# Gateloop attention and a low-rank mixer: the first pair's second layer by half products, three pairs' inputs turned by DMA, chunk products joined, a new order

## The chip, the cores and the metric

One core of one Trainium2 chip runs the whole kernel. The metric is the device time of one launch in microseconds (us); smaller is better. TensorE is PE, VectorE is DVE, ScalarE is ACT, GpSimd is POOL, and SyncE (SP) issues most of the DMAs.

## The reference

Attention first: per batch and head a complex state decays by a normalised gate and takes up k v at every time step; the output is q times the state's real part. Then the mixer: a product of low rank along the sequence is added, and a two-layer net with a relu is added to that.

```python
# q, k, v, a_re, a_im: (4, 8, 768, 48)      B, H, S, D
mag = np.sqrt(a_re * a_re + a_im * a_im)
scale = np.minimum(mag, 0.999) / (mag + 1e-06)
a_re_n, a_im_n = (a_re * scale, a_im * scale)
for t in range(S):
    new_re, new_im = ar * S_re - ai * S_im, ar * S_im + ai * S_re
    S_re, S_im = (new_re + kv, new_im)            # kv = k[t] v[t]
    y[:, :, t] = np.einsum('bhd,bhde->bhe', q[:, :, t], S_re)
x = y.transpose(0, 2, 1, 3).reshape(4, 768, 384)
h = x.transpose(0, 2, 1) @ U @ V                  # rank 32 along the sequence
u = x + h.transpose(0, 2, 1)
out = u + np.maximum(u @ w_ch1, 0.0) @ w_ch2      # 384 -> 1536 -> 384
```

## The kernel before

**Tiling.** The 768 time steps of each of the four batches are six chunks of 128 rows, 24 chunks in all; a group is two chunks. The mixer works on pairs of two chunks (256 rows), 12 pairs in all, numbered m = 0 to 11.

**Attention.** For each chunk `gates`, `angles` and `waves` turn the gate into decays; they are mostly PE prefix sums, ACT functions and DVE products. `prep` weighs q and k and turns them: chunks 0 to 5 by PE transposes, later ones in `cross`, where ACT splits the numbers into 16-bit halves, SP writes them to DRAM (L933) and a DMA transpose fetches them back (L934). `chain` holds the chunk's PE products: `products` (L956) within 64 rows, masked by DVE (L959); `state` (L976), which makes the state's increments; `inside` (L1005), the masked products with v; and `before` (L1013), q with the carried state, in two halves. `products` and `before` use one arrangement of the PE array, `state` and `inside` another, and the mixer's large matmuls the whole array. ACT copies the result to a tile `xo` of 128 x 384 (L1022, L1024). `again` (L665) loads the gate a second time for a check of its range: each chunk's a_re and a_im by a DMA of its own (L671), one ACT square, two DVE operations, whose outcome goes into the tile `low` (L661).

**Mixer.** In `mixer(m)`, once in each batch, `rank` (L1048) multiplies the six chunks by U, and for every pair `spread` (L1071) multiplies that by V and `mixed` adds it to xo on DVE. `turned` transposes each chunk on PE (L1087, three 128 x 128 transposes) and copies it to uT (L1091). Pair 0 is worked ahead: its first layer is made without the low-rank part (`up`, L1102) and then mended by `corrected` (PE L1142, DVE L1148, from a tile `more` that ACT copies). From pair 2 on, the first layer is `up_fewer` (L1214), a scheme with fewer products; its combined weights come from `combine` (DVE L1267) and its combined inputs from DVE additions L1186.

**Second layer.** Pair 0 uses `down` (L1303): for each of its two chunks 12 matmuls of 128x384, each of which needs one piece of w2, and one DVE addition. The others use `down_two` (L1346): with the rows and columns split into halves it takes seven half products instead of eight, 42 matmuls of 128x192, eight DVE sums over the hidden layer (L1338) and seven additions (L472), and it reads three differences of w2's halves. These three (W2S, DVE L652) can only be made when all of w2 has been converted from its 64-bit form (`single`, DVE L616, L624, L472). One half of w2 is overwritten by a difference, "turned w2" (L1416), ahead of the first pair's use of it.

**Order.** All operations are registered with a `Plan`; a hand-written table `ORDER` of their numbers then sets the order of issue on every engine. `SPARE` puts dummy matmuls (`idle`, L1506) before an operation, `WARM` others (`warm`, L1513). They write to banks that nothing reads yet. An engine works off its instructions strictly in this order.

Of the kernel before, what the change touches and what calls it, by code (L numbers as in the profile page):

```python
# [118 lines left out]
)  # L119

SPARE = {
    410: 3, 447: 1,
}

WARM = {
    112: (2, 1), 126: (1,), 136: (2, 2, 2, 2, 2, 2, 1), 141: (2,), 162: (2, 2, 2), 235: (2, 2, 2, 2, 1), 242: (2,), 245: (2,), 259: (2, 2, 1), 266: (1, 1, 1, 1, 1, 1, 1, 1, 1),
}

AIM = {}

DUMP = None

# [194 lines left out]
def kernel(  # L327
# [24 lines left out]
    KH = KF // 2  # L352
    DH = DM // 2

    PLAIN = 1
    NS = 5
    FEWER, SINGLE, AHEAD = 2, 3, 1
    NCH = S // CH
# [69 lines left out]
    def c_act(n):  # L428
        return 0.22 + 0.0008 * n
# [1153 lines left out]
```

## Time and profile before

| | us |
|---|---|
| median of 3 runs (lowest, highest) | 530.15 (529.94, 530.81) |
| the profiled execution, its time | 529.77 |
| its span, first to last instruction | 528.0 |

The profile lists for each engine the time it was busy as a share of the span, then the span in 40 slices, the DMA queues, the chain of work that ended last, and the costliest groups of instructions. The program's names in a row stand as output<-inputs. A matmul of 32-bit floats leaves two records in the trace, one for each of its passes, so the counts of PE records in the trace are twice the matmuls in the code. Where a time of one matmul is given it holds both. The table by windows gives the busy time of each engine within stretches of the span; a share of PE below the stretch's length is time in which PE stood still.

### The profile page before, as it was taken

The numbers are of one execution on the slowest core, as the hardware profiler recorded it, in microseconds if no ns is written. First come the engines' busy times: TensorE is split into PE (matmuls) and PEld (weight loads), VectorE is DVE, ScalarE is ACT, GpSimd is POOL, SyncE is SP. The second block draws the span as 40 slices with busy tenths as digits, with TensorE's granted clock in tenths as the row PEclk, the third lists the DMA queues.
The fourth block names the chain that finished last, engine by engine and source line by source line (L and its number), as shares of the span: only waits on it lengthen the run. The fifth ranks groups of instructions, "written<-read, shape, count | busy, mean of one in ns | idle before, by whom it ended". The sixth has DMA issues, their size and how long they took to land.

```text
span 528.0 us, 15692 instructions
## 1 busy us (share of the span) xinstructions
PE 509.3 (96%) x6670; PEld 460.3 (87%) x6670; DVE 414.5 (79%) x787; ACT 346.0 (66%) x555; POOL 31.6 (6%) x61
## 2 busy tenths in 40 slices
PE   4999999899999999999999999999999999999996
PEld 2777887666998997999999989999999989999996
DVE  4779897799989987898798797878796575958452
ACT  8899998998869978978896768843543313131100
POOL 1000000001010000101011000110000000000110
PEclk9999999999999999999999999999999999999998
DMA  9959958479999998999899958999897543333101
GB/s 226 173 115 270 209 115 191 140 138 217 197 215 244 216 215 145 204 217 202 205 198 227 210 144 175 170 242 229 192 217 178 108 90 61 76 60 61 39 32 35
DMA packets 280670, 87.06 MB, mean 165 GB/s; under 512 B 271288, under 2 KB 272784, under 8 KB 280592
## 3 DMA queue, kind: packets, MB, share of 16 engines
q1 hardware_dynamic: 278384, 81.63, 76.0%
q0 software_dynamic: 2208, 4.35, 2.4%
q8 instruction: 54, 0.88, 0.7%
q14 instruction: 24, 0.20, 0.1%
HBM read 43.03 MB, written 23.63 MB: 126 GB/s over the span
## 4 chain that ended last, share of the span: by engine, by line
PE 88%; ACT 5%; DMA 3%; DVE 2%; issue 1%; SPq 0%; ACTq 0%
PE down L1346 25%; PE few L1214 14%; PE bank L1214 11%; PE up L1102 6%; PE inner L956 4%; PE bank L1013 4%; PE bank L976 4%; PE down L1303 3%; PE bank L1005 2%; DMA gate<-F 2%; PE bank L1071 2%; PE bank L1087 2%; ACT gate L466 1%; PE bank L777 1%; PE bank L782 1%; PE bank L842 1%
## 5 line engine op out<-in xcount | busy, mean ns | idle before, releaser
L466 ACT ACTIVATE gate<-gate 128x768 f32<-128x768 f32 (+2 forms) x85 | 86.1, 1018 | 25.8 <-DMA gate<-in_a_im_dram 14.7
L1346 PE MATMUL down<-w,h 128*128 128x192 f32 x396 | 70.4, 328 | 0.0
L466 ACT ACTIVATE QK<-QKC 128x768 uint16<-128x768 uint16 (+1 forms) x72 | 58.5, 848 | 13.1 <-DVE QKC L469 7.9
L1346 PEld LDWEIGHTS down<-w,h 128*128 128x128 f32 x396 | 64.6, 190 | 1.2 <-issue 0.8
L469 DVE TENSOR_TENSOR QKC<-qk,cs 128x768 f32<-128x768 f32 x48 | 44.9, 952 | 1.0 <-ACT cs L466 0.6
L472 DVE TENSOR_TENSOR xo<-down,xo 128x192 f32<-128x192 f32 (+1 forms) x79 | 29.9, 385 | 14.3 <-PE down L1346 14.1
L1222 ACT COPY h<-few 128x512 f32<-128x512 f32 x35 | 20.2, 583 | 27.8 <-PE few L1214 27.6
L1222 ACT COPY h<-bank 128x512 f32<-128x512 f32 x25 | 14.3, 588 | 36.0 <-PE bank L1214 31.0
L1346 PE MATMUL down<-stage 128*128 128x192 f32 x198 | 37.2, 328 | 0.0
L1102 PE MATMUL up<-uT,w 128*128 128x256 f32 x144 | 33.8, 383 | 0.0
L1346 PEld LDWEIGHTS down<-stage 128*128 128x128 f32 x198 | 32.5, 190 | 0.3 <-issue 0.2
L1102 PEld LDWEIGHTS up<-uT,w 128*128 128x128 f32 x144 | 26.7, 190 | 4.9 <-issue 0.6
L1290 POOL DMA_DIRECT2D out_dram<-xo x32 | 18.5, 590 | 202.9 <-DVE xo L472 164.5
L463 ACT ACT_TABLE_LOAD x22 | 28.2, 1283 | 1.1 <-PEq L1567 0.7
L828 POOL DMA_DIRECT2D gate<-F x15 | 12.0, 797 | 274.7 <-DVE stage L616 86.3
L1226 DVE CUSTOM_DVE_ANT_1 h<-few,h 128x512 f32<-128x512 f32 x31 | 21.0, 686 | 8.8 <-PE few L1214 8.1
L1214 PE MATMUL few<-extra,w 128*128 128x128 f32 x216 | 27.8, 275 | 0.0
L956 PE MATMUL inner<-QK 112*64 112x64 f32 x768 | 27.5, 224 | 0.2 <-DVE AT L959 0.2
L466 ACT ACTIVATE cs<-F 128x384 f32<-128x384 f32 x48 | 24.4, 518 | 3.9 <-DVE F L851 3.7
L956 PEld LDWEIGHTS inner<-QK 112*64 112x64 f32 x768 | 24.5, 138 | 2.4 <-issue 0.8
L1214 PEld LDWEIGHTS few<-extra,w 128*128 128x128 f32 x216 | 26.3, 192 | 0.1
L466 ACT ACTIVATE es<-bank 128x384 f32<-128x384 f32 x44 | 18.4, 502 | 9.2 <-PE bank L777 8.2
(185 smaller groups left out, 1166.8 us busy)
## 6 DMA issues: line engine op xcount, KB each, us to landing
xd<-QK SPq DMA_DIRECT2D x36, 512.0 KB
gate<-in_a_re_dram SPq DMA_DIRECT2D x48, 192.0 KB
gate<-in_a_im_dram SPq DMA_DIRECT2D x48, 192.0 KB
stage<-in_moe_w_ch_dram SPq DMA_DIRECT2D x12, 768.0 KB
qk<-in_q_dram SPq DMA_DIRECT2D x24, 192.0 KB
qk<-in_k_dram SPq DMA_DIRECT2D x24, 192.0 KB
VP<-in_v_dram SPq DMA_DIRECT2D x24, 192.0 KB
out_dram<-xo POOLq DMA_DIRECT2D x12, 192.0 KB, 4.2
```

The lines of the kernel that those rows point to most:

```text
L463: ACT(1.37, rank, lambda: nc.scalar.preload_act_table_set(name), writes=[TABLE])
L466: return nc.scalar.activation(out=o, in_=i, func=f, **kw)
L469: nc.vector.tensor_tensor(out=o, in0=a, in1=b, op=OP.mult)
L472: nc.vector.tensor_tensor(out=o, in0=a, in1=b, op=OP.add)
L956: nc.tensor.matmul(out=get(*ps0)[r:r + HC, h], lhsT=k_of(h, r, HC), rhs=q_of(h, r, HC), start=True, stop=True, tile_position=(0, r))
L976: nc.tensor.matmul(out=get(*dk[r])[x:x + D, h], lhsT=get(*ks)[at, h, x // DP, 0:D], rhs=get(*VPi)[at, h], start=True, stop=True, tile_posi ...
L1013: nc.tensor.matmul(out=get(*y[u])[side(r, u), p], lhsT=q_of(h, r * HC, HC), rhs=get(*(mid_G if r else ("G", i - 1)))[:, h], start=False, s ...
L1102: nc.tensor.matmul(out=get(*ps)[:, e], lhsT=w1[:, f, (ff + e) * 128:(ff + e + 1) * 128], rhs=get(*uT)[:, f], start=(f == 0), stop=(f == KD ...
L1214: nc.tensor.matmul(out=get(*ps)[:, q], lhsT=w()[:, q * 128:(q + 1) * 128], rhs=v[0](), start=(n == 0 and q == 0), stop=True, skip_group_ch ...
L1222: ACT(c_act(n3 * CH) - 0.045, RU, lambda i=i, k=k: nc.scalar.copy(out=at(i, k), in_=get(*ps)), [ps], [o])
L1226: DVE(c_dve(n3 * CH), RU, lambda i=i, k=k: nc.vector._custom_dve(dve_ops.TENSOR_ADD_SAT, out=at(i, k), in0=get(*ps), in1=at(i, k), s0=math ...
L1346: nc.tensor.matmul(out=get(*to)[:, part], lhsT=x(j), rhs=y[:, j], start=(first and j == 0), stop=(j == KH - 1), skip_group_check=not first)
```

## The change

1. `PLAIN` goes from 1 to 0: pair 0's second layer is made by `down_two` as well.
2. `TURNED = (9, 10, 11)`: for the chunks of the last three pairs `across` takes the place of PE's transposes and ACT's copy. ACT splits xo into 16-bit halves (two operations a chunk, into one tile `XU` that all six chunks share in turn), SP writes 192 KB to DRAM, and a DMA transpose brings it back into uT.
3. `JOIN = 8`: from chunk 8 on, a chunk's `state` is issued in one piece with the chunk before's `inside`, and the chunk before's two `before` halves in one piece with the chunk's `products`. The first chunk of each batch is left out, and 14 are joined. The numbers of matmuls stay.
4. `again` loads a group's two chunks by one DMA for a_re and one for a_im, 24 in place of 48, with 768 floats in a row for each partition; before, the rows were of 48. `low` holds 16-bit numbers; that makes room for `XU`.
5. `spread` no longer reads uT; the transposes take its buffer.
6. `ORDER`, `SPARE` and `WARM` are new: nine single dummies in place of four, and fewer but wider ones in `WARM`.

Line numbers move: `down_two`'s matmuls are at L1406, its sums at L1398, W2S at L653, "turned w2" at L1476, `spread` at L1116, `up_fewer` at L1274, the `combine` of weights at L1327, its inputs at L1246, the write and the transpose of `across` at L1150 and L1151, the loads of `again` at L674, the dummies at L1562, L1566 and L1573.

```diff
-    5, 97, 96, 0, 1, 2, 3, 102, 99, 101, 103, 4, 104, 105, 106, 107, 98, 116, 100, 115, 117, 118, 119, 10, 154, 8, 111, 112, 16, 9, 230, 108, 231,
...
+    5, 96, 0, 1, 2, 3, 4, 97, 99, 101, 102, 103, 104, 105, 100, 115, 98, 116, 117, 106, 8, 9, 111, 107, 108, 118, 119,
...
 SPARE = {
-    410: 3, 447: 1,
+    388: 1, 410: 1, 416: 1, 462: 3, 669: 3,
 }
 WARM = {
-    112: (2, 1), 126: (1,), 136: (2, 2, 2, 2, 2, 2, 1), 141: (2,), 162: (2, 2, 2), 235: (2, 2, 2, 2, 1), 242: (2,), 245: (2,), 259: (2, 2, 1), 266: (1, 1, 1, 1, 1, 1, 1, 1, 1),
+    125: (3,), 136: (4, 4, 4, 1), 141: (2,), 162: (4, 4, 4, 2, 2), 167: (2, 2, 2), 187: (1,), 235: (2, 2, 2, 2, 1), 263: (2, 2, 1), 273: (2,),
 }
-    PLAIN = 1
+    PLAIN = 0
+    JOIN = 8
-    low = singles.tile([128, GC * DM], FP, name="low")
+    low = singles.tile([128, GC * DM], U16, name="low")
+    XU = singles.tile([128, 2, DM], U16, name="XU")
+    TURNED = (9, 10, 11)
# again
-        for (nm, src), i in ((a, i) for a in ((ar, a_re), (ai, a_im)) for i in range(lo, hi)):
-            SP(c_dma(DM), ("load", 30 + n), lambda nm=nm, src=src, i=i: nc.sync.dma_start(out=get(*nm)[:, i - lo], in_=rows(src, i)),
-               writes=[nm + (i,)])
+        for nm, src in ((ar, a_re), (ai, a_im)):
+            SP(c_dma(W), ("load", 30 + n), lambda nm=nm, src=src: nc.sync.dma_start(
+                out=flat4(nm), in_=src[b, :, c * CH:(c + hi - lo) * CH].rearrange("h t d -> h (t d)").rearrange("h (p m) -> h p m", m=W)), writes=[nm])
# chain
+        joined, joins = c > 0 and i >= JOIN, not last and i + 1 >= JOIN
...
+        if joined:
+            p_inside, p_in, p_y, p_befores, p_b, p_leaves, p_rooms, p_takes = pending.pop(i - 1)
+            p_rooms()
+            def fused_x():
+                state(0, H)
+                p_inside()
+            PE(1.3, RR, fused_x, [ks, VPi] + p_in, [dk[r] for r in parts_k] + p_y, way=3, steps=4 * H * len(parts_k) + 4 * H,
+               takes=[mid_G] + p_takes)
+            states(True)
+            def fused_y():
+                p_befores()
+                products()
+            PE(1.8, RR, fused_y, p_b + [QK], p_y + [ps0], takes=[ATi], way=1, steps=8 * H)
+            states(False)
+            kept()
+            p_leaves()
# mixer
-            PE(0.76, R0, products, [r, ("V", 0)] + [uT + ("kept",)] * (m >= AHEAD), ps, way=5, steps=8)
+            PE(0.76, R0, products, [r, ("V", 0)], ps, way=5, steps=8)
+            if m in TURNED:
+                across(cc, i, u)
+                return
-            PE(0.33, R0, turn, [u], [tr], steps=KD)
+            PE(0.33, R0, turn, [u], [tr], takes=[uT], steps=KD)
+        def across(cc, i, u):
+            xu, xv = ("xu", i), ("xv", i)
+            ring(xu, "xu", [XU])
+            buffer(xv, "XV", 6, [CH, DM], bass.MemoryType.DRAM)
+            for n in range(2):
+                ACT(c_act(DM), R0, lambda n=n: act(get(*xu)[:, n], get(*u).bitcast(U16).rearrange("p (m n) -> p m n", n=2)[:, :, n], AF.Copy),
+                    [u], [xu + (n,)])
+            SP(0.6, R0, lambda: nc.sync.dma_start(out=get(*xv).bitcast(U16), in_=get(*xu).rearrange("p n m -> p (n m)")), [xu], [xv])
+            SP(0.8, R0, lambda: nc.sync.dma_start_transpose(
+                out=get(*uT).rearrange("p f (c t) -> p f c t", c=MC)[:, :, cc].bitcast(U16),
+                in_=get(*xv).bitcast(U16).rearrange("t (n m) -> (t n) m", n=2)), [xv], [uT + (cc,)])
```

**DVE, around the three differences of w2** (L652 before, L653 after; w_77 and w_78 are w2, w_76 and, after, w_77 are w1). Before:

```order
L472 ISA w_77<-w_77,stage 128x1536
L469 TENSOR_TENSOR QKC_107<-qk,cs 128x16x48
L469 TENSOR_TENSOR QKC_103<-qk,cs 128x16x48
L652 TENSOR_TENSOR stage<-w_77 128x1152
L469 TENSOR_TENSOR qk<-qk,es 128x768
L836 CAST GS_96<-gate 128x384
L837 TENSOR_TENSOR GS_97<-gate,GS_96 128x384
L652 TENSOR_TENSOR stage<-w_77,stage 128x1152
L472 TENSOR_TENSOR xo<-down,xo 128x384
L736 ISA gate<-gate 128x768
L798 TENSOR_TENSOR least<-least,T_115 112x16
L652 TENSOR_TENSOR stage<-w_77,stage 128x1152
```

And now:

```order
L471 ISA w_78<-w_78,stage 128x1536
L653 TENSOR_TENSOR stage<-w_78 128x1152
L838 CAST GS_97<-gate 128x384
L839 TENSOR_TENSOR GS_98<-gate,GS_97 128x384
L653 TENSOR_TENSOR stage<-w_78,stage 128x1152
L853 SCALAR_TENSOR_TENSOR F<-F,bank_62 128x384
L653 TENSOR_TENSOR stage<-w_78,stage 128x1152
L468 TENSOR_TENSOR QKC_108<-qk,cs 128x16x48
L1398 TENSOR_TENSOR stage<-extra 128x384 x2
L468 TENSOR_TENSOR QKC_104<-qk,cs 128x16x48
L1398 TENSOR_TENSOR more<-stage,extra 128x384
L1398 TENSOR_TENSOR stage<-stage,extra 128x384
```

Behind the last converted piece of w2 there were eight other rows between it and the third difference; now there are three, and pair 0's first four sums follow soon after.

**PE, at pair 0's second layer** (extra holds its hidden layer, stage and more hold differences and sums). Before:

```order
L1303 MATMUL down<-w_77,extra 128x384 x6
L842 MATMUL bank_61<-GS_96,prefix_r 128x384
L842 MATMUL bank_61<-GS_97,prefix_r 128x384
L1303 MATMUL down<-w_77,extra 128x384 x14
```

And now, with the 12 rows ahead of the first wait for a difference:

```order
L1562 MATMUL bank_62<-ident 128x128 x3
L844 MATMUL bank_62<-GS_97,prefix_r 128x384
L844 MATMUL bank_62<-GS_98,prefix_r 128x384
L1162 MATMUL up<-uT,w_77 128x256 x6
L1406 MATMUL down<-w_78,extra 128x192 x12
L1406 MATMUL down<-stage,extra 128x192 x6
L1406 MATMUL down<-stage 128x192 x3
L1406 MATMUL down<-stage,more 128x192 x3
L1406 MATMUL down<-stage 128x192 x6
```

The matmuls that read stage need the differences and the sums; those that read w_78 and extra alone do not.

**PE, behind the last batch's `spread`** (few and bank are `up_fewer`'s outputs for pairs 8 and 9). Before:

```order
L1071 MATMUL bank_65<-r,V 128x192
L1346 MATMUL down<-w_77,h 128x192 x3
L1346 MATMUL down<-stage,h 128x192 x3
L1346 MATMUL down<-stage 128x192 x3
L1346 MATMUL down<-stage,h 128x192 x3
L1087 MATMUL bank_61<-ident,xo 128x128 x3
L1346 MATMUL down<-stage,more 128x192 x3
L1087 MATMUL bank_62<-ident,xo 128x128 x3
L1346 MATMUL down<-stage 128x192 x3
L1346 MATMUL down<-w_77,h 128x192 x6
L1214 MATMUL bank_63<-extra,w_76 128x128 x4
```

And now:

```order
L1116 MATMUL bank_62<-r,V 128x192
L1274 MATMUL few<-extra 128x128 x4
L1406 MATMUL down<-w_78,h 128x192 x9
L1406 MATMUL down<-stage,h 128x192 x3
L1406 MATMUL down<-w_78,h 128x192 x3
L1406 MATMUL down<-stage,h 128x192 x3
L1406 MATMUL down<-stage 128x192 x3
L1406 MATMUL down<-stage,more 128x192 x3
L1406 MATMUL down<-stage 128x192 x6
L1406 MATMUL down<-w_78,h 128x192 x3
L1406 MATMUL down<-w_78,stage 128x192 x3
L1406 MATMUL down<-w_78,more 128x192 x3
```

The whole second layer of pair 8, 42 matmuls, now stands between the last `spread` and pair 9's first layer, which follows it; the transposes are gone.

More of the change, by code (lines that the diff above doesn't have):

```diff
@@ L1015, in before, with befores, rooms, halves @@
                                      tile_position=(0, (r ^ u) * HC), skip_group_check=True)
-        PE(0.44, RR, inside, [VPi, ATi, mid_G] + ([("G", i - 1)] if c else []), y, way=3, takes=[xi], steps=4 * H)
+        def befores():
+            for r in range(0 if c else 1, 2):
+                before(r)
+        def rooms():
+            for r in range(2):
+                psum(y[r], "Y", [128, HH, D], [128, HH, CH])
+            buffer(xi, "xo", 8, [128, DM])
+        def halves(a):
+            return a.rearrange("p (a u d) -> p a u d", u=2, d=D)
@@ new lines, in leaves @@
+        def leaves():
+            ACT(c_act(HH * D) - 0.04, RR, lambda: nc.scalar.copy(out=halves(get(*xi))[:, :, 0], in_=get(*y[0])), [y[0]], [xi + (0,)])
+            for r in range(2):
+                ACT(c_act(HH * D) + 0.04, RR, lambda r=r: nc.scalar.copy(out=halves(get(*xi))[r * HC:(r + 1) * HC, :, 1],
+                                                                         in_=get(*y[1])[side(r, 1)]), [y[1] + (r,)], [xi + (r + 1,)])
+        b_in = [QK, mid_G] + ([("G", i - 1)] if c else [])
@@ new lines, in chain @@
+        psum(ps0, "A", [128, H, HC])
+        buffer(mid_G, "GM", 2, [DQ, H, D])
+        if not last:
+            buffer(G, "G", 2, [DQ, H, D])
+        for r in parts_k:
+            psum(dk[r], "Y", [128, H, D], [128, H, DP])
+        if joined:
[14 more added lines that the diff above has]
+            p_leaves()
+        else:
+            PE(0.947, RL, products, [QK], [ps0], takes=[ATi], way=1, steps=4 * H)
+            kept()
+            for h0 in (0, HH):
+                PE(0.443, RR, lambda h0=h0: state(h0), [ks, VPi], [dk[r] + (h0,) for r in parts_k], way=3,
+                   steps=4 * HH * len(parts_k),
+                   takes=[mid_G] + ([] if last else [G]))
+            states(True)
@@ L1017, in chain @@
+        if joins:
+            pending[i] = inside, y_in, y, befores, b_in, leaves, rooms, [xi]
+            return
+        rooms()
+        PE(0.44, RR, inside, y_in, y, way=3, takes=[xi], steps=4 * H)
         if c:
@@ L1019, in chain @@
         PE(0.467, RR, lambda: before(1), [QK, mid_G], [y[0] + (1,), y[1] + (1,)], way=1, steps=2 * H)
-        def halves(a):
-            return a.rearrange("p (a u d) -> p a u d", u=2, d=D)
-        ACT(c_act(HH * D) - 0.04, RR, lambda: nc.scalar.copy(out=halves(get(*xi))[:, :, 0], in_=get(*y[0])), [y[0]], [xi + (0,)])
-        for r in range(2):
-            ACT(c_act(HH * D) + 0.04, RR, lambda r=r: nc.scalar.copy(out=halves(get(*xi))[r * HC:(r + 1) * HC, :, 1],
-                                                                     in_=get(*y[1])[side(r, 1)]), [y[1] + (r,)], [xi + (r + 1,)])
+        leaves()
+    pending = {}
     def mixer(m, ahead=False):
@@ L1082, in turned @@
             u = ("xo", i)
+            if m in TURNED:
+                across(cc, i, u)
+                return
             tr = out_of("uTp", i, [128, KD, CH], [128, 4, CH])
```

51 lines of the change are left out of this document (22 added, 29 removed), and 171 rows, old and new, of the table ORDER.

## The prediction

> **What bounds the kernel now.** I read the page's busy times and its chain first, then windows, then the waits of PE. On the page, the share of each engine and the chain of work that ended last:
>
> ```profile
> PE 509.3 (96%) x6670; PEld 460.3 (87%) x6670; DVE 414.5 (79%) x787; ACT 346.0 (66%) x555; POOL 31.6 (6%) x61
> PE 88%; ACT 5%; DMA 3%; DVE 2%; issue 1%; SPq 0%; ACTq 0%
> ```
>
> The windows (length, then busy PE, PEld, DVE, ACT, POOL with their counts, granted clock, DMA share, GB/s), first three that make up the span, then four around the first pairs:
>
> ```profile
> 0.00:24.00 24.00, 15.64 (x80) 11.10 (x81) 14.18 (x31) 19.06 (x35) 1.94 (x14) 1.00 1.08 209
> 24.00:504.00 480.00, 474.46 (x6463) 430.52 (x6462) 389.56 (x734) 326.90 (x521) 28.09 (x44) 1.00 0.81 169
> 504.00:528.00 24.00, 19.17 (x132) 18.72 (x130) 10.80 (x23) 0.00 (x0) 1.60 (x3) 0.94 0.11 37
> ...
> 114.00:130.00 16.00, 16.00 (x150) 9.86 (x139) 15.20 (x24) 13.11 (x17) 1.35 (x2) 1.00 0.82 216
> 130.00:147.00 17.00, 17.00 (x130) 14.94 (x130) 16.34 (x27) 15.46 (x25) 0.78 (x1) 1.00 0.89 175
> 147.00:164.00 17.00, 15.89 (x296) 14.79 (x289) 15.20 (x32) 12.56 (x18) 1.91 (x3) 1.00 1.13 263
> 164.00:180.00 16.00, 15.97 (x263) 15.16 (x262) 15.26 (x30) 15.74 (x28) 1.07 (x2) 1.00 1.11 210
> ```
>
> PE bounds the middle 480 us: only 5.5 us of it are idle. The head (8.4 us idle) and the tail (4.8) are bound by something else. From 114 to 180 DVE is as full as PE (62.0 of 66 us), so there work given to DVE can cost what PE saves. Two of PE's waits (us in all, times, longest):
>
> ```profile
> PE up L1142 <- ACT more L1128: 2.1, 1, 2.1
> PE down L1346 <- DVE xo L472: 1.1, 1, 1.1
> ```
>
> Both, 3.2 us together, lie before 165 and are most of what a better order could win in the middle.
>
> **The first pair's second layer on PE.** Three pieces of the chain (start, length, count of records; a matmul is two records):
>
> ```profile
> 108.77 2.59 PE up L1102 x12
> ...
> 118.86 9.03 PE down L1303 x28
> ...
> 211.74 1.95 PE down L1346 x12
> ```
>
> A matmul of 128x384 takes 2 x 9.03/28 = 0.645 us, one of 128x192 takes 2 x 1.95/12 = 0.325. Removed are 24 x 0.645 = 15.48, added 42 x 0.325 = 13.65: **-1.83 us**.
>
> **Transposes.** From the timeline of PE (start, length):
>
> ```profile
> 431.63 0.49 PE L1087 MATMUL bank<-ident,xo 128*128 128x128 f32 x3
> 431.96 1.14 PE L1346 MATMUL down<-stage,more 128*128 128x192 f32 x6
> ```
>
> Three hold PE for 431.96 - 431.63 = 0.33 us, 0.11 each; by the row's own length, which the next row overlaps, 0.49/3 = 0.163. Eighteen fewer (72 to 54): **-2.0 us**, at most -2.9. ACT loses six copies and gains twelve splits, but in the last batch it has room.
>
> **Joining.** The number of matmuls stays; what falls is the number of changes between arrangements of the array, by my count of the orders from 153 to 143.
>
> ```profile
> 165.74 0.68 PE L1005 MATMUL bank<-VP,AT 64*64 64x48 f32 x32
> 166.35 0.67 PE L1013 MATMUL bank<-G,QK 112*64 112x48 f32 x16
> 166.85 0.64 PE L1013 MATMUL bank<-GM,QK 112*64 112x48 f32 x16
> 167.42 1.16 PE L1214 MATMUL few<-gate,w 128*128 128x128 f32 x8
> ...
> 416.76 1.15 PE L1005 MATMUL bank<-VP,AT 64*64 64x48 f32 x64
> 417.84 0.67 PE L1013 MATMUL bank<-GM,QK 112*64 112x48 f32 x16
> ```
>
> One block of 32 records lasts 0.61 us to the next start, a double block of 64 lasts 1.08, 0.14 less than twice 0.61; the second of the two L1013 halves, which leaves its arrangement, lasts 0.57, the first 0.50. So one change costs 0.07 to 0.14; with 0.10, ten make **-1.0 us** (-0.7 to -1.4). The price: `inside` of a chunk now goes out with the next chunk's `state`, so a chunk's output leaves a chunk later. From chunk 8 on the pairs stand far behind the chunks, and I take nothing for that.
>
> **Dummies.** Five more single ones. Three before (six records) held PE from 111.53 to 112.29:
>
> ```profile
> 111.53 0.83 PE L1506 MATMUL up<-ident 128*128 128x128 f32 x6
> 112.29 1.26 PE L1142 MATMUL up<-V,more 32*128 32x256 f32 x4
> 114.37 4.14 PE L1303 MATMUL down<-w,extra 128*128 128x384 f32 x12
> ```
>
> That is 0.25 each, at most +1.3. Most stand at the correction of pair 0, where PE waited 2.1 for ACT: I take 0. The new `WARM` lies in the head, where PE has 8.4 us free: 0. The sum on PE is -4.8.
>
> **DVE's side.** Pair 0 gains eight sums and its additions become halves. Does PE wait for the differences of w2? DVE's timeline:
>
> ```profile
> 115.14 0.41 DVE L1148 CUSTOM_DVE_ANT_0 extra<-up,extra 128x256 f32<-128x256 f32 x1
> ...
> 119.98 0.95 DVE L472 CUSTOM_DVE_ANT_0 w<-w,stage 128x1536 uint16<-128x1536 uint16 x1
> ...
> 128.28 1.35 DVE L652 TENSOR_TENSOR stage<-w,stage 128x1152 f32<-128x1152 f32 x1
> ```
>
> Before, the third difference ended at 129.63, long after pair 0's layer began at 114.37. In the new order, priced row by row, 3.55 us more PE work stands ahead of that layer, so it begins near 117.9. Its first 12 matmuls (3.9 us) need no difference, the next 6 need the third one (at 121.8), and those after them, at 123.75, the first sums, which DVE ends 4.1 us behind the third difference. So the third difference must end by 119.65. On DVE it now follows the last correction by 5.9 us of work (one conversion, three differences, three other rows). On PE 12 first-layer matmuls (2 x 2.59 by the chain's row), a `state` (0.87) and two prefix sums (0.46, both in rows further down), 6.5 us without dummies, stand between its last correction and the layer, so that correction ends near 111.4; DVE ran it up to 2.85 us late before (115.14 against 112.29). That gives 111.4 + 2.85 + 5.9 = 120.15, 0.5 late, and the six dummies that stand there now would take more than that anyway: I take 0. The upper bound is today's 129.63 less the 5.65 us of DVE rows that were moved behind it: 124.0, which would stop PE for 4.3 us.
>
> The next place is pair 2's first `few`, which reads a weight that DVE combines:
>
> ```profile
> 152.89 0.55 DVE L1338 TENSOR_TENSOR h<-h 128x384 f32<-128x384 f32 x1
> 153.36 0.55 DVE L1186 TENSOR_TENSOR extra<-uT 128x384 f32<-128x384 f32 x1
> ...
> 157.37 0.36 DVE L836 CAST GS<-gate 128x384 fp32r<-128x384 f32 x1 [1.59 <-DMA gate<-F]
> ...
> 159.17 0.68 DVE L1267 TENSOR_TENSOR w<-w,extra 128x512 f32<-128x512 f32 x1
> ```
>
> ```profile
> 161.46 0.94 PE L976 MATMUL bank<-VP,QKC 64*48 64x48 f32 x64
> 162.33 1.15 PE L956 MATMUL inner<-QK 112*64 112x64 f32 x32
> 163.41 0.62 PE L842 MATMUL bank<-GS,prefix_r 128*128 128x384 f32 x2
> 163.87 1.95 PE L1214 MATMUL few<-extra,w 128*128 128x128 f32 x16
> ```
>
> Today the weight ends at 159.85 and PE comes at 163.87: 4.0 us to spare. In the new order a whole chunk's products move behind this point (0.87 for `state`, 1.08 for `products`, 0.61 and 1.07 for the rest, from the rows above: 3.63), and 1.83 is saved, so PE comes at 158.4. DVE has eight sums (0.47 each by the starts) and five half additions (0.27, a little over half of that) more ahead, and about 1.8 us of other rows less: 159.85 + 3.3 = 163.1. If both hold, PE stands 4.7 us; if DVE's idle gaps close (50 - 46.74 = 3.3 in the windows from 114 to 164, 1.59 of it in the row above) it is 1.4; if they close further, nothing. I take the middle, **+2.2 us** handed back.
>
> **Turned inputs.** Is pair 9's input back in time? Rows of SP's timeline, its longest kind of wait (us in all, times, longest), and ACT's copy of 384 columns, whose mean of 476 ns stands for one split:
>
> ```profile
> 400.94 0.34 SPq L933 DMA_DIRECT2D xd<-QK  x1
> ...
> 405.08 4.71 SPq L934 DMA_TRANSPOSE QK<-xd  x2
> ...
> SPq L671 <- DVE low L661: 48.6, 10, 9.2
> ...
> L1091 ACT COPY uT<-bank 128x384 f32<-128x384 f32 x21 | 9.6, 476 | 16.3 <-PE bank L1087 16.3
> ```
>
> The write of 512 KB was followed by its transpose after 4.14 us; 192 KB is 3/8 of it, 1.6 us; a transpose is 3/8 of 2.36 to issue and, by the same share, some 2.5 us to land. Addition 0.55, two splits 1.0, write 1.6, the second chunk's splits 1.0 (they wait for the shared tile) and write 1.6, transpose 2.5, DVE's combined inputs 1.5 (nine additions, most of them a third of the one at 153.36): 9.7 us. On PE 4 `few` matmuls (eight records, 0.9 by the sixteen at 163.87) and 42 downs (13.65) stand in between, 14.6. Behind a write that waits for its split, SP holds only loads of `again` and the other turned chunks. So it is hidden; without that cover it would cost 9.7, once, since pairs 10 and 11 are turned in the shade of pair 9. The 24 fewer loads of `again` only free DMA engines and SP; nothing on PE's path waits for them.
>
> **The sum.** 529.77 - 4.8 + 2.2 = 527.2 for the profiled execution. The median lies 0.38 above that execution: **527.5 us**. The bounds: dummies +1.3, the hand-back 0 to 4.7, transposes -2.9, changes -0.7 to -1.4 give 525 to 530 for this case.
>
> **The rivals.**
>
> *The new order also fills PE's old waits.* For it: 3.2 us of them lie exactly where the order is rewritten and where dummies now stand. Against it: DVE is full there. With the hand-back at nothing too, 529.77 - 4.8 - 3.2 + 0.38 = 522.2.
>
> *DVE hands everything back.* The stop at pair 2's first `few` takes the whole 4.7: 529.77 - 4.8 + 4.7 + 0.38 = 530.1, no change. For it are the full windows of DVE; against it its idle gaps.
>
> *The first pair waits for all of w2: slower.* `down` could begin at 114.37 with a part of w2; `down_two` cannot go past its twelfth matmul without the last piece. The point from which this outweighs the gain is a third difference later than 119.65 + 2.6 = 122.2. With 124.0 the stop is 4.3: 531.8; with today's 129.63 it is 10: 537.5. Against it is the order, which pulls the differences forward. By the Trainium skill ("TensorE: Matmul & The Clock Gate", "What's actually happening") an idle window of some 3.4 us halves the clock until PE has been busy as long again; a stop of that length would then cost about 1.7 us more, by an estimate from that page. The trace neither confirms nor denies it in the middle: the granted clock is 1.00 in every window of it.
>
> *The turned inputs come late: slower.* If a load of `again` stands ahead of the write on SP and waits for DVE as it did, 9.2 us, the chain is 18.9 against 14.6: +4.3, 531.8. For it: these loads are mixed among the writes on SP. Against it: the mean of the ten such waits is 4.9, and 9.7 + 4.9 is just the cover.
>
> **How the numbers follow.** Forecast 0.44 (527.5), old waits filled 0.23 (522.2), everything handed back 0.10 (530.1), w2 late 0.13 (531.8 and more), turned inputs late 0.10 (531.8). The range 521.0 to 532.0 leaves out the far half of the w2 case and a little on either side. A measurement can tell 0.2%, 1.06 us: faster is below 529.1, slower above 531.2. Faster: 0.42 of the forecast, all 0.23: 0.65. Same: 0.02 of the forecast, 0.06 of handing back, 0.02 of the two late cases: 0.10. Slower: the other 0.25.
>
> **What would show it.** In the new profile L1303 is gone and L1406 has 1008 records; the transposes have 54; PE's busy time falls by about 5 us apart from dummies. A wait of PE at L1406 on DVE's stage near 121 would show w2 late, one at the first L1274 DVE's hand-back, one on L1151 near the last batch's start the turned inputs. The forecast fails if PE's waits before 165 grow by more than 5 us, or vanish.

## The result and the profile after

The changed kernel takes 544.63 us (median of 6 runs, 543.23 to 545.81) against 530.13 for the kernel before (528.60 to 530.81, 6 runs): a ratio of 1.0275, 95% interval 1.0253 to 1.0296. It is 14.5 us slower; 527.5 was predicted. The profiled execution took 545.36, with a span of 543.5. Times here are medians; where one execution was slow as a whole (one each of the experiments e1, e3 and n8), it is left out.

From the page: busy times, shares of the chain of waits, and the clock granted to PE in 40 slices.

```profile
PE 514.4 (95%) x6680; PEld 465.6 (86%) x6680; DVE 419.2 (77%) x800; ACT 349.8 (64%) x561; POOL 32.2 (6%) x62
PE 71%; ACT 10%; DMA 7%; DVE 7%; issue 2%; SPq 1%; DVEq 0%; ACTq 0%
PEclk9999999979999999999999999999889999999999
```

The counts came as forecast: L1406 has 1008 records, two for each of its 504 matmuls, and the transposes (L1135) have 54, one each. PE's busy time should have fallen by about 5 us; it rose from 509.3 to 514.4, in part because matmuls take longer at a lower clock. Its share of the chain fell from 88% to 71%, DMA's rose from 3% to 7%, ACT's from 5% to 10%. Three slices have a clock below 9 tenths, in two places. PE's waits (us in all, times, longest):

```profile
PE bank L784 <- DVE GL L744: 8.1, 1, 8.1
PE bank L1274 <- ACT h L1282: 4.8, 1, 4.8
PE few L1274 <- ACT h L1282: 2.0, 1, 2.0
PE bank L1116 <- ACT r L1099: 1.8, 1, 1.8
PE up L1566 <- DVE extra L1208: 1.6, 2, 1.4
PE down L1406 <- DVE xo L471: 1.5, 1, 1.5
PE bank L976 <- DMA VP<-in_v_dram: 0.8, 1, 0.8
```

The first is the head and belongs to both kernels. Of the others, one is the correction of pair 0 (L1566, at 110.8), one the wait for `r` (L1116, at 210) and one at L1406 lies at 474. The two on ACT's `h`, at L1274, and the one on `VP` lie between 375 and 394. Windows of that stretch (length; busy PE, PEld, DVE, ACT, POOL with counts; clock; DMA share; GB/s):

```profile
360.00:384.00 24.00, 21.02 (x420) 19.20 (x419) 18.55 (x42) 9.13 (x16) 2.55 (x4) 1.00 1.09 226
384.00:408.00 24.00, 19.23 (x271) 18.80 (x270) 15.28 (x26) 8.39 (x17) 0.00 (x0) 0.86 0.76 158
408.00:432.00 24.00, 24.00 (x289) 23.62 (x287) 15.42 (x36) 8.39 (x16) 1.62 (x3) 1.00 0.60 161
```

The first two of them in the kernel before:

```profile
360.00:384.00 24.00, 24.00 (x353) 23.72 (x347) 20.37 (x42) 10.55 (x19) 1.07 (x2) 1.00 0.93 198
384.00:408.00 24.00, 24.00 (x373) 23.65 (x362) 18.66 (x41) 9.39 (x18) 1.62 (x3) 1.00 0.93 197
```

PE is idle for 2.98 and 4.77 us in the first two, where it was full before. What the stop at 389 waits for is on the chain (start, length):

```profile
375.88 4.23 DMA VP<-in_v_dram
...
382.97 9.28 DMA gate<-in_a_im_dram
392.25 0.02 issue
392.27 0.02 ACT gate L465
...
393.02 0.57 ACT h L1282
393.60 0.04 issue
393.64 2.07 PE bank L1274 x8
```

A second gate load of `again` (384 KB) is issued at 382.97 and lands 9.28 us later. ACT, in order, stands at its square from 386.8; behind the square stands the copy of `h` for which PE waits. So a range check that no result needs until the end holds up the mixer's first layer. The same eight matmuls of L1274 then last 2.07 us, twice the 1.05 of their neighbours: PE had been granted half its clock.

The other place of a low clock is the correction of pair 0. PE's timeline, then the windows around it (columns as above):

```profile
112.20 1.65 PE L1566 MATMUL up<-ident 128*128 128x128 f32 x6 [1.40 <-DVE extra L1208]
113.64 4.81 PE L1162 MATMUL up<-uT,w 128*128 128x256 f32 x12
```

```profile
110.00:112.00 2.00, 0.81 (x6) 0.30 (x4) 1.57 (x3) 2.00 (x5) 0.76 (x1) 0.74 0.02 1
112.00:114.00 2.00, 1.79 (x7) 1.78 (x8) 2.00 (x5) 2.00 (x4) 0.00 (x0) 0.50 0.00 0
114.00:116.00 2.00, 2.00 (x6) 1.57 (x5) 1.97 (x3) 2.00 (x4) 0.00 (x0) 0.50 0.49 98
116.00:118.00 2.00, 2.00 (x6) 1.61 (x6) 1.97 (x4) 1.65 (x2) 0.00 (x0) 0.55 0.93 292
118.00:120.00 2.00, 2.00 (x74) 1.61 (x72) 0.21 (x1) 0.00 (x0) 0.00 (x0) 1.00 1.11 318
```

At a stop of 1.40 us the clock falls to 0.50, by the windows' means from 111.0 to 117.8. The first layer's 12 matmuls take 4.81 us; before, the same 12 took 2.59.

### The profile page after: what moved, and what is told of

The parts are those of the page before. It is cut to its first block, busy times and chain, and to the rows that moved or that the text cites. A ratio compares the mean times of both kernels' runs of the same rounds, so it can differ in the third digit from the quotient of the medians.

```text
span 543.5 us, 15715 instructions
## 1 busy us (share of the span) xinstructions
PE 514.4 (95%) x6680; PEld 465.6 (86%) x6680; DVE 419.2 (77%) x800; ACT 349.8 (64%) x561; POOL 32.2 (6%) x62
## 4 chain that ended last, share of the span: by engine, by line
PE 71%; ACT 10%; DMA 7%; DVE 7%; issue 2%; SPq 1%; DVEq 0%; ACTq 0%
PE down L1406 28%; PE few L1274 12%; PE bank L1274 9%; PE up L1162 4%; DMA gate<-in_a_im_dram 3%; PE bank L1008 3%; PE inner L964 3%; ACT gate L465 3%; PE bank L976 3%; PE bank L1000 2%; DVE QKC L468 1%; ACT L462 1%; DMA gate<-in_a_re_dram 1%; ACT es L465 1%; ACT xy L465 1%
## 5 line engine op out<-in xcount | busy, mean ns | idle before, releaser
L1406 PE MATMUL down<-w,h 128*128 128x192 f32 x396 | 69.6, 328 | 0.0
L1406 PEld LDWEIGHTS down<-w,h 128*128 128x128 f32 x396 | 64.5, 190 | 0.8 <-DVE xo L471 0.3
L471 DVE TENSOR_TENSOR xo<-down,xo 128x192 f32<-128x192 f32 (+1 forms) x84 | 31.6, 381 | 24.6 <-PE down L1406 24.4
L1406 PE MATMUL down<-stage 128*128 128x192 f32 x216 | 39.8, 328 | 1.5 <-DVE xo L471 1.5
L1406 PEld LDWEIGHTS down<-stage 128*128 128x128 f32 x216 | 35.6, 190 | 2.6 <-DVE xo L471 1.8
L1162 PE MATMUL up<-uT,w 128*128 128x256 f32 x144 | 36.3, 402 | 0.2 <-ACT extra L465 0.2
L1162 PEld LDWEIGHTS up<-uT,w 128*128 128x128 f32 x144 | 28.2, 201 | 6.0 <-issue 0.8
L1274 PE MATMUL few<-extra,w 128*128 128x128 f32 x216 | 28.4, 278 | 0.2 <-DVE xo L471 0.2
L1274 PEld LDWEIGHTS few<-extra,w 128*128 128x128 f32 x216 | 26.0, 192 | 1.1 <-DVE xo L471 0.5
L1286 DVE CUSTOM_DVE_ANT_1 h<-bank,h 128x512 f32<-128x512 f32 x29 | 19.5, 687 | 9.5 <-PE bank L1274 7.3
```

The source lines that it names most:

```text
L471: nc.vector.tensor_tensor(out=o, in0=a, in1=b, op=OP.add)
L1162: nc.tensor.matmul(out=get(*ps)[:, e], lhsT=w1[:, f, (ff + e) * 128:(ff + e + 1) * 128], rhs=get(*uT)[:, f], start=(f == 0), stop=(f == KD ...
L1274: nc.tensor.matmul(out=get(*ps)[:, q], lhsT=w()[:, q * 128:(q + 1) * 128], rhs=v[0](), start=(n == 0 and q == 0), stop=True, skip_group_ch ...
L1286: DVE(c_dve(n3 * CH), RU, lambda i=i, k=k: nc.vector._custom_dve(dve_ops.TENSOR_ADD_SAT, out=at(i, k), in0=get(*ps), in1=at(i, k), s0=math ...
L1406: nc.tensor.matmul(out=get(*to)[:, part], lhsT=x(j), rhs=y[:, j], start=(first and j == 0), stop=(j == KH - 1), skip_group_check=not first)
```

## The experiments

Theories that the expectations name by letters. **A**: squares of `again` now stand right behind their loads in the order, so ACT waits for DMA. **B** and **D** are A's rivals: something else waits at the same places (B), or the clock halves whatever PE waits for (D). **C** (C'): the loads themselves come among the last chunks' writes, transposes and `VP` loads, and make these and themselves late; of this, **C1** is through their places in SP's order, **C2** through the bytes that they move. Each kernel is the changed one with one edit unless said otherwise; times are medians. Places are numbers in `ORDER`.

**Squares later (A).** All squares and range operations go some 20 to 50 places back; of the seventh group, for example:

```diff
 # a_re and a_im loads; square; two range operations
-1884, 1886; 1887; 1885, 1888
+1885, 1886; 1924; 1925, 1926
```

> The changed kernel; only the range check's square on ACT and its two operations on DVE stand some 25 to 40 places later in the order, behind work that PE waits for. Theory A (the second load of the gate is not back when ACT and DVE come to it; both stand in order, so the copies of `few` behind the square come late and PE stops twice, 2.0 and 4.8 us near 376 and 389, and then runs some 6 us at half clock): these stops and the drop of the clock near 391 go, 10 to 11 us, so about 534 us. Theory B (the stops are the price of the joined order or of DMA engines that are full, and something else will wait in the same place): 541 us or more.

568.8 us, ratio 1.068 (1.060 to 1.076): 24 us worse than the change, where A had about 534. A's cure is wrong. The same edit with the corrections first (e4, below) has these waits of SP and PE:

```profile
SPq L674 <- DVE low L662: 29.6, 4, 9.6
```

```profile
PE down L1406 <- DVE h L1286: 7.1, 1, 7.1
PE inner L964 <- DMA QK<-xd: 6.0, 1, 6.0
PE bank L976 <- DMA VP<-in_v_dram: 4.5, 1, 4.5
```

With later range operations the buffers come free later, SP waits 29.6 us for them ahead of loads (10.7 in the changed kernel), and the transposes and `VP` loads behind them come late.

**The loads' shape.**

```diff
-            SP(c_dma(W), ("load", 30 + n), lambda nm=nm, src=src: nc.sync.dma_start(
-                out=flat4(nm), in_=src[b, :, c * CH:(c + hi - lo) * CH].rearrange("h t d -> h (t d)").rearrange("h (p m) -> h p m", m=W)), writes=[nm])
+            SP(c_dma(W), ("load", 30 + n), lambda nm=nm, src=src: [nc.sync.dma_start(out=get(*nm)[:, i - lo], in_=rows(src, i)) for i in range(lo, hi)], writes=[nm])
```

> The changed kernel with its own order; each load of `again` is made as two loads of 192 KB in runs of 192 bytes, as before. Theory A (the place in the order counts, not the load's shape): within 3 us of the changed kernel, 542 to 548. Theory C (the wide load is slow to come back by its shape): the two stops go, about 534.

545.56 us (1.029, 1.023 to 1.035). Rows of 192 or of 3072 bytes make no difference here.

**Corrections first.** In DVE's order the four corrections of pair 0 go ahead of their neighbours:

```diff
 L1141 COPY uT<-bank_61 128x3x128
+L1208 ISA extra<-up,extra 128x256 x4
 L471 TENSOR_TENSOR xo<-bank_63,xo 128x384
-L1208 ISA extra<-up,extra 128x256 x2
 L471 TENSOR_TENSOR xo<-bank_62,xo 128x384
 L468 TENSOR_TENSOR QKC_104<-qk,cs 128x16x48
-L1208 ISA extra<-up,extra 128x256
 L625 TENSOR_SCALAR w_78<-w_78 128x768
 L468 TENSOR_TENSOR QKC_106<-qk,cs 128x16x48
-L1208 ISA extra<-up,extra 128x256
```

> The changed kernel; on DVE the last four corrections of pair 0 go ahead of two additions of `mixed` and one product of `prep` (2.05 us of DVE work). Theory A (PE stands 2 us between 110 and 113 for DVE's corrections, and that stop brings the half clock from 110.8 to 117.2, some 3.3 us more): 4 to 5 us less, about 540. Rival D (the clock halves there whatever PE waits for): at most 2 us less, 543 or more, and the granted clock near 115 stays at 0.5.

PE's timeline of this kernel:

```profile
111.81 0.94 PE L1566 MATMUL up<-ident 128*128 128x128 f32 x6 [0.51 <-DVE extra L1208]
112.58 2.76 PE L1162 MATMUL up<-uT,w 128*128 128x256 f32 x12
115.32 0.94 PE L976 MATMUL bank<-VP,QKC 64*48 64x48 f32 x64
```

The stop shrinks to 0.51, the clock stays at 1.00, the 12 matmuls take 2.76 and the next work comes at 115.32 instead of 118.38. The end does not gain: 544.0 us (1.022, 1.014 to 1.030), where A had about 540. At 332 us the two kernels are level again, and the stops from 370 on follow.

The clock does not follow the stop at every execution. Run n7 (below) has the stop of the changed kernel at full clock, and e4 the short stop with half clock; their rows, first n7's:

```profile
113.21 0.94 PE L1566 MATMUL up<-ident 128*128 128x128 f32 x6 [1.39 <-DVE extra L1208]
113.98 2.75 PE L1162 MATMUL up<-uT,w 128*128 128x256 f32 x12
```

```profile
111.23 1.60 PE L1566 MATMUL up<-ident 128*128 128x128 f32 x6 [0.51 <-DVE extra L1208]
112.62 3.80 PE L1162 MATMUL up<-uT,w 128*128 128x256 f32 x12
```

In the eleven profiles of the new order with a stop of 1.2 to 1.4 us here, the clock falls to 0.50 within the stop in ten, for 3.4 us or twice that; in the six with the stop of 0.51 us it falls in one. So the shorter stop makes the half clock rarer and does not rule it out.

**Both.** 

> Both edits of the order together (squares late, corrections first). Theory A: the two gains add up, 14 to 16 us, about 529 to 531. Theory B and D: 539 or more.

 563.55 us (1.062, 1.055 to 1.069). That is 5.3 below e1, but the executions of the two overlap (560.7 to 566.9 here, 562.7 to 569.6 there).

**Without the second loads.** Loads, squares and range operations of `again` become nothing; done to the changed kernel (n1) and to the one before (n2).

```diff
-        ACT(c_act(W), R1, lambda: act(flat4(ai), flat4(ai), AF.Square), [], [ai])
+        ACT(c_act(W), R1, lambda: None, [], [ai])
...
```

> The changed kernel without `again`: the second load of the gate, its square on ACT and its two operations on DVE are left out, for all groups; the rest keeps its order. Theory A (where the check's pieces stand in the new order makes PE stop for ACT's copies): the stops of `few` near 376 and 389 and the half clock behind them go, 11 us: 533 to 535. Theory B (those copies or the DMAs around them would be late anyway): 540 or more.

> The kernel before without `again` in the same way. Theory A: in the old order the check lies in the shade of PE, so 528.5 to 530.5, no more than 1.5 us less. Theory B' (the check costs PE some us in either order, by SP and DMA): 525 or less.

The changed kernel falls to 533.05 (1.003, 1.000 to 1.006), by 11.6 us; against the kernel before as it ran beside each of them (530.13 and 531.13), the loss falls from 14.5 to 1.9 us, by 12.6. The kernel before stays at 531.23 (1.000, 0.998 to 1.003). So the same work that cost nothing in the old order costs 11.6 us or a little more in the new one. Windows of the kernel before without it, then of the changed one without it (columns as above):

```profile
360.00:384.00 24.00, 24.00 (x314) 23.49 (x311) 17.20 (x37) 10.89 (x20) 1.07 (x2) 1.00 0.57 123
384.00:408.00 24.00, 24.00 (x420) 23.60 (x416) 16.16 (x36) 7.65 (x15) 1.62 (x3) 1.00 0.60 151
408.00:432.00 24.00, 24.00 (x326) 21.51 (x325) 11.50 (x21) 4.72 (x11) 0.00 (x0) 1.00 0.18 36
```

```profile
360.00:384.00 24.00, 24.00 (x454) 23.16 (x453) 17.29 (x37) 9.88 (x18) 2.34 (x4) 1.00 0.98 212
384.00:408.00 24.00, 24.00 (x307) 23.76 (x306) 16.84 (x38) 7.99 (x17) 0.88 (x2) 1.00 0.49 118
408.00:432.00 24.00, 24.00 (x361) 21.67 (x361) 10.35 (x19) 7.18 (x17) 0.74 (x2) 1.00 0.06 23
```

In the old order the other transfers fill the DMA engines to 0.57 and 0.60 there; in the new one they come earlier and closer together, 0.98 in the first window and 0.06 in the last. A pair of transposes that goes out at 385.6 in the old order goes out at 378.8 in the new one. The turned inputs have no part in it: their first write goes out at 429.6. Room for the check's loads is left after 384, but those of this stretch go out before it.

**The loads alone.** Squares and range operations are left out, loads stay. 

> The changed kernel with the loads of `again`, but without the square and the two DVE operations. Theory A (ACT and DVE stand behind a load that is not back): as without `again`, 532 to 536. Theory C' (the loads themselves, 9 MB on DMA engines and on SP's queue, make other transfers late): near the changed kernel, 541 or more.

 541.51 us (1.018, 1.013 to 1.022): the loads alone cost 8.5 of the 11.6, as C' had it (541 or more; A had 532 to 536). With no square there is no copy behind one; PE waits for `QK` transposes (3.4 us in three) and `VP` (2.0) instead.

**Other places.** Two groups' squares later (n4), all of the check behind the last chunk's transposes (n5), and all of it where the old order had it, counted in PE's instructions (n7). The fourth group:

```diff
 # a_re and a_im loads; square; two range operations
-1737, 1758; 1759; 1767, 1769
+1749, 1758; 1772; 1774, 1777    n4
+1872, 1871; 1896; 1899, 1901    n5
+1773, 1774; 1787; 1781, 1790    n7
```

> The changed kernel, complete; only the third and fourth group's square and DVE operations stand 13 to 20 places later, so that no load of a later group has to wait longer for its buffer. Theory A: most of the 11 us go, 534 to 538. Theory B: 542 or more.

> The changed kernel, complete, with all of the second gate loads, their squares and the two DVE operations behind each moved in the table to places 1775 to 2165: behind the last chunk's turned loads, one group about every 33 places. If the loads cost by standing in SP's order ahead of the last chunks' transposes and `VP` loads (theory C), the time falls from 544.6 to what the kernel without the second load took, 533, within 2 us, and the waits PE `bank` on DMA `VP` and PE on ACT `h` after 375 us go. If the loads cost wherever they stand, because they take DMA engines or ACT time (rival), it stays at 540 or more. If the end now waits for the squares, the last matmul stays near its time and the span's end moves.

> The changed kernel, complete; only the second gate loads, squares and range operations take other positions: those that they had in the old order, counted in PE's instructions ahead of them (for the fourth to seventh group the square moves 28 to 62 places behind its loads; nothing else moves by more than 25 places). If the place of the loads in the new order is the cause (theory C), the stops of PE after 370 us shrink to those of the old order and the time falls to 533 to 537. If any place for them now costs, since the new order has less slack for anything on SP and ACT there (rival), it stays at 541 or more, with other waits in place of the old ones.

n4: 543.62 us (1.022, 1.017 to 1.027), n5: 559.34 (1.056, 1.052 to 1.060), n7: 559.11 (1.054, 1.052 to 1.057). Theory A had 534 to 538 for n4: the two stops on `h` are gone there, but PE stops for 6.3 us between 378 and 410 for `VP`, for DVE's `xo` and `h` and for ACT's copy to `xo`. Theory C had 533 for n5 and 533 to 537 for n7; both missed by over 20 us. In n5 the stops before 400 are gone, but the first one behind it has this chain:

```profile
404.11 0.32 SPq L674
404.48 6.94 DMA gate<-in_a_re_dram
411.44 0.96 DVE gate L661
412.40 0.48 DVE xo L471
412.93 3.52 PE few L1274 x16
```

The load takes 6.94 us, DVE stands at the range operation for it, behind that stands an addition of `xo`, and PE stops for 7.3 us. I gave some 20 to 30 places between a load and the operations on it; PE stops seven more times up to the end, 11.0 us in all, each time for DVE. In n7 the window from 360 to 384 holds both the loads and the earlier transfers, with a DMA share of 1.11. PE stops for 1.8 us there, less than in the changed kernel, but for 2.6 us at 344 and for 10.0 from 408 to 504, where the changed kernel stops for 1.5. The places of the old order do not bring back its slack. With the corrections first, n5 and n7 stay the same within their spread:

> The same, with the first pair's corrections ahead of the neighbouring work on DVE and ACT (as in e3). In e3 this took 1.7 us up to the first few-column product of pair 2, which the later waits ate. If those waits came from the loads, the gain is now kept: 1 to 3 us below the run with the late loads alone, 530 to 532, equal to or just below before (530.1). If the corrections' gain is eaten by something else, the two are equal within 0.7 us.

> The same, with the first pair's corrections ahead of the neighbouring work on DVE and ACT (as in e3). If the first theory holds, 1 to 3 us below the run before it, 531 to 535; if later waits eat the gain as in e3, equal to it within 0.7 us.

561.38 us (1.057, 1.051 to 1.063) and 557.25 (1.052, 1.050 to 1.053).

**Another queue (C1).** The loads go out from POOL's queue; in the changed kernel (n9), with the corrections first (n11), and, as a control, in the kernel before (n12).

```diff
-            SP(c_dma(W), ("load", 30 + n), lambda nm=nm, src=src: nc.sync.dma_start(
+            POOL(c_dma(W), ("load", 30 + n), lambda nm=nm, src=src: nc.gpsimd.dma_start(
```

> The changed kernel, complete; the second gate loads go out from POOL's queue instead of SP's, at the same places of the table. Theory C1 (the loads cost by standing in SP's order, where they hold up the transposes and the `VP` loads behind them and are held up themselves): the pairs of transposes are issued in some 5 us instead of 8, PE's stops after 370 us go and the time falls to 533 to 537. Theory C2 (they cost by filling the DMA engines beside the transposes, from whatever queue): within 3 us of 544.6, with the transposes still long. Had POOL's own work (outputs, sums for the state) to wait behind the loads, PE or the end would wait for POOL, and the time is above 544.6.

> The loads from POOL's queue and the corrections first, both complete. If C1 holds, 1 to 4 us below the run with POOL's queue alone, 530 to 535. If C2 holds, 541 to 545 as in e3.

> The kernel before with its second gate loads from POOL's queue: a control for the queue itself. In the old order these loads cost nothing (531.2 without them, 530.1 with). If POOL's queue costs nothing by itself, 529 to 531.5; if issuing from POOL holds up POOL's outputs or sums, above 532, and the run with POOL's queue in the new order is to be read against that.

551.45 us (1.037, 1.032 to 1.043), 551.39 (1.035, 1.029 to 1.042) and, for the control, 543.87 (1.020, 1.013 to 1.028). The queue costs the old order 13 us by itself: ACT waits 25.0 us for these loads there (14.7 in the kernel before), most likely since they stand behind POOL's outputs and its sums for the state. These three say nothing on C1. The control shows that the slack of the old order does not survive this queue either.

**Bytes (C2).** Every instruction stays at its place; only the columns that the loads bring change, to a half (n13) and a sixteenth (n14).

```diff
-                out=flat4(nm), in_=src[b, :, c * CH:(c + hi - lo) * CH].rearrange("h t d -> h (t d)").rearrange("h (p m) -> h p m", m=W)), writes=[nm])
+                out=flat4(nm)[:, 0:W // 2], in_=src[b, :, c * CH:(c + hi - lo) * CH].rearrange("h t d -> h (t d)").rearrange("h (p m) -> h p m", m=W)[:, :, 0:W // 2]), writes=[nm])
```

> The changed kernel with every instruction at its place, but each second gate load brings only the first half of its columns (192 KB for 384; squares and range operations run on the whole tile, half of it old data, so half of the second check is left out). Theory C2 (the loads cost by the time that they take on the DMA engines, which the new order has already filled from 360 to 384 us): about half of the 11.6 us goes, 538 to 541. Theory C1 (they cost by their places in SP's order and by the waits tied to them, whatever their size): 543 or more.

> The same with a sixteenth of the columns (24 KB). C2: 533 to 536, close to the kernel without the second load (533), the squares on ACT and the range operations on DVE, which stay, costing the rest. C1: 543 or more. If the squares and range operations cost by themselves, what is left above 533 is their price.

The old data in the rest of each tile lay out of range, so both kernels went on to the program's general path behind the usual one and took 8970 and 8969 us; those times say nothing on the change. The usual path stands whole in their traces, up to its last matmuls. Their last rows there, first for the changed kernel, then without the check (n1), with half of the bytes and with a sixteenth:

```profile
537.32 1.14 PE L1406 MATMUL down<-w,more 128*128 128x192 f32 x6
```

```profile
524.77 1.14 PE L1406 MATMUL down<-w,more 128*128 128x192 f32 x6
```

```profile
526.21 1.14 PE L1406 MATMUL down<-w,more 128*128 128x192 f32 x6
```

```profile
527.25 1.14 PE L1406 MATMUL down<-w,more 128*128 128x192 f32 x6
```

Half the bytes take away 537.32 - 526.21 = 11.1 of the 12.6 us between the first two; a sixteenth takes away no more. (These are one profile each; the executions of the changed kernel differ by up to 2.6 us, those without the check by up to 5.9.) C2 had half of the cost for half of the bytes, so it was right on the cause and wrong on the size. SP's order, the squares and the range operations are all still there. From 330 to 500 us ACT's waits for these loads (first the changed kernel, then half the bytes) shrink with them:

```profile
ACT gate L465 <- DMA gate<-in_a_im_dram: 29.9, 9, 6.7
```

```profile
ACT gate L465 <- DMA gate<-in_a_im_dram: 12.6, 4, 4.5
```

That decides for C2 against C1: with every place kept, the loss comes and goes with the bytes. It does not make places free: n5 and n7 moved the same bytes and lost 15 us more. The loads' bytes alone are not enough for a loss, as the old order shows. That it takes a stretch which other transfers have filled fits the shares without the check (0.57 and 0.98), but was not tried by itself; with the check, the kernel before has a share of 0.93 there and does not stop.

**Corrections first, without the second loads.** 

> The changed kernel without the second load of the gates and the range check (left out as in n1) and with the first pair's corrections ahead of the neighbouring work (as in e3). If the remaining loss of n1 (533.0 against 531.2 for the old order without the same work) is the stop and the half clock at 110 to 118 us, which e3 removed, the time falls by 2 to 4 us to 529 to 531, so that the change then gives a gain against 531.2. If the gain gets lost later even without the loads, within 1 us of 533.0.

 531.28 us (1.001, 0.999 to 1.003), 1.8 below n1 (1.2 when each is read against the kernel before beside it), level with the kernel before and with n2 (531.23). The clock of its profile is 0.999. So the two together account for the loss of 14.5 us to within about 1 us; the second is no larger than the spread of such runs. No kernel that was tried beats the one before.

## Why the prediction was wrong

**The step that failed.** "The 24 fewer loads of `again` only free DMA engines and SP; nothing on PE's path waits for them." Priced at nothing, the check with them is 11.6 us, 8.5 by its loads alone. I counted issues, where the bytes stayed the same, and did not ask what the new order put beside them. Transposes and `VP` loads of the last chunks go out earlier in the new order; the DMA share from 360 to 384, without the check, goes from 0.57 to 0.98. Part of the warning was there: the windows of the kernel before had a DMA share of 0.93 in that stretch. How small the slack was could not be read from its waits, since ACT's four waits for these loads, 1.0 to 7.0 us, all lie between 412 and 483. The sign of failure that the prediction named, PE's waits before 165, did not show the loss either: they fell from 3.2 to 1.4 us, and the loss lies at 375 to 398. The rival "turned inputs come late" saw loads among the writes on SP but put them before the wrong work.

**The correction of pair 0** was priced at nothing (its dummies at 0, at most +1.3). DVE's new order puts its corrections behind other work. In the profiles the stop of 1.40 us and the half clock with it put PE 3.06 us behind e3 (118.38 against 115.32); 2.1 of them are the clock (the 12 matmuls in 4.81 us, 2.75 in n7 with the same stop). At the end 1.2 to 1.8 are left of it (n1 to n10), within what one pair of medians can tell.

**First pair's second layer**, -1.83: held. Summed from each PE record's start to the next one's, L1303's 15.2 us are gone and L1406 has 13.4 more, with the 1.5 us stop at 474 in it.

**Transposes**, -2.0: L1135's sum is 3.8 below L1087's; 2.1 of that is a stop that stood behind one of them before, so 1.7 is theirs. Held.

**Joining**, -1.0: not seen. By the same sums of n10, `state` falls by 1.5, `products` rise by 1.1 and the `before` halves by 0.6, `inside` stays. Fewer changes of arrangement give nothing that these sums show.

**Dummies** took 2.6 us more in n10, not 0, with a stop of 0.7 behind three of them in it. Three others stand behind pair 0's last correction; they wait for it themselves (the stop of 0.51) and put the work behind them off by 0.77 (e3: 111.81 to 112.58).

**DVE's hand-back**, +2.2: pair 2's first `few` comes at 162.3, and PE does not wait for DVE there. The stop and the half clock at 110 are in it; without the half clock, in n10, it comes at 159.6. By the sum it would have been 160.6 (158.4 and 2.2), with everything handed back 163.1; before it was 163.9. Nothing was handed back there. The old waits of that stretch (2.1 and 1.1) went, and the wait for `r` at 210 grew from 0.6 to 1.8.

**The rivals.** Old waits filled: right on the two waits, but the time did not follow. Late differences of w2: no wait of PE on them, fallen. Turned inputs late: DVE waits 0.6 us for them once, fallen as put. Half clock: by the Trainium skill ("TensorE: Matmul & The Clock Gate", "What's actually happening") it takes an idle window of some 3.4 us; here half the clock came with a stop of 1.40 us, after gaps under 0.2 us, and in e4 with one of 0.51, and the measurement decides.

**What stays open.** Which part of the new order moved the transfers of the last chunks (the joined products, or the table itself) was not tried. Why four other sets of places of the check (e1, n4, n5, n7) never did better than 543.6 was read only from their waits; whether a place exists with room on the DMA engines and enough distance from a load to its square was not shown. What ate the rest of the 4.8 us in n10 was only summed by line (joining, dummies, the wait for `r`, and 2.3 us more from the matmuls of `up_fewer`), not tried one by one.

## What to carry to other kernels

Work off the critical path is free only as long as the engine that it shares has room at that time: before an order is changed, list what runs in the background in each stretch and read that stretch's DMA share with and without it, since a stretch that goes from 0.57 to 0.98 takes the room of the background work. Count a transfer's bytes and the in-order queue of whoever waits for it, not its issues: here a check needed only at the end stood on ACT ahead of a copy that PE needed at once. To price such work, leave it out of both kernels: the difference of the two (0 and 11.6 us) found in two runs what the waits alone had not told.

## What was not expected of the hardware

- PE's clock halved without a long stop, and not at every execution. In the changed kernel's profile it was 0.50 from 111.0 to 117.8, around a stop of 1.40 us that began at 110.8, and from 390.8 to 397.7, in and behind the stop of 4.77 us (from the windows 390 to 392 and 396 to 398, 0.71 and 0.58). Both last 6.8 to 6.9 us. In e4 it came for 3.4 us with a stop of 0.51, and in n2 for 3.4 us from 96.6, when a stop of 2.14 us had been over since 95.1. But stops of 1.39 us in n7, of 2.10 at 94 in the kernel before and of 1.97 at 375 in the changed one left it at 1.00. The length of the one stop does not decide it.
- A load of 384 KB took 9.28 us to land, with a mean DMA share of 1.08 meanwhile; half of that size ended nearly all the stops, so the cost is far from proportional to the bytes.
- Rows of 192 or of 3072 bytes of these loads made no difference to the kernel's time (545.56 against 544.63 us).
